# Top-32 attention with a PReLU layer on one core: four of nine selection masks on the scalar engine, output normalisation on GpSimd

## The chip, the core and the metric

The kernel runs on one core of one Trainium2 chip. A core has a matrix engine (PE, with PEld for its weight loads), a vector engine (DVE), a scalar engine (ACT), GpSimd (POOL) and a sync engine (SP) whose queue starts most transfers. Each engine works through its own list of instructions in order and waits on semaphores for the others. The metric is device time in microseconds (us): of several runs the median, and of one profiled run the trace.

## The reference, cut to what matters

```python
# q, k, v: (8, 8, 576, 64); tokens 4608, model width 512, hidden width 2048
scores = scale * q @ k^T                      # per batch and head, 576 x 576
kth    = 32nd largest score of each row
attn   = softmax(where(scores >= kth, scores, -1e9))
x      = (attn @ v) gathered to (4608, 512)
h      = x @ w_in
out    = (max(h, 0) + alpha * min(h, 0)) @ w_out
```

So each row of scores keeps its 32 largest entries; the rest get weight zero. The sum in the softmax is the sum of the kept exponentials, and a common factor on a row's kept weights falls out of the division.

## The kernel before, in words

Two heads make a **pair**: 32 pairs, four to a batch. A pair has nine score tiles of 128 rows by 576 columns (eight full ones, `j` 0 to 7, and `j` 8 that holds the last 64 rows of both heads). The 288 tiles are run by a loop written out by hand over **ticks**; tick `n` starts tile `n`, and in the same tick older tiles get their later steps. All five engines are ordered by this loop, with no scheduler behind it (`tc.manual_schedule`).

A tile's way through the engines:

- PE computes the scores into PSUM (L320). ACT copies them to SBUF with a per-row guess of the threshold subtracted (`b`, L329), then takes their sign with a running sum (`h`, L335; the sum `S_all` counts how many scores lie above the guess), and the exponential (`e`, L340), for two tiles at once where they come in twos.
- GpSimd turns the count into a sign word (`SG`, L345), one tick later. DVE flips the tile by it (`y`, L351), so that the wanted border lies among the small values, finds the eight largest of each of six segments (`C`, L361, two ticks after the tile's start), merges these to the 24 largest (`L`, L376 and L378, a tick later), and once for three tiles picks one of the 24 by rank (`sel_eq`, `sel_pr`, `sel_sum`; the rank comes from `sel_a`, L384, a square on ACT). `limit` (L405) turns it into the row's limit `KP`.
- Seven ticks after its start (`LAG_W`), a tile gets its mask on DVE (`mk = b >= KP`, L425). GpSimd multiplies mask and exponential to the weights (`w`, L435). SP transposes two tiles of weights at once by DMA (`wT`, L448).
- PE multiplies the transposed weights with v (`pu`, L486; `v` has a column of ones, so one column is the softmax sum): rows of `j` 0 to 3 as group 0, the rest as group 1. DVE takes the reciprocal of the sum (`rz`), and ACT writes the normalised outputs (`av_out`, L515): four activations of 64 columns for group 0, six for group 1. SP transposes those into `xT` (`x_turn`), and the hidden layer (L689 to L712) takes them from there, one step per tick.

Within a tick, DVE's order is: the masks, the held sum of a selection, the segments of one tile interleaved with the merge of another, small steps of the preparation of a later pair, `limit` every third tick, and last the flip of the tile before. GpSimd's order is: weights, then `SG`, then what the tick has at its end, among which are four DMA issues for `v` per pair (`load_v`, L149). A flip therefore needs the `SG` that GpSimd issues behind the weights of the same tick.

The masks use one buffer, the two-tile `b` five, the two-tile `e` four, `w2` three, `wT` six. The last four pairs run in another order of tiles with rules of their own.

## Time and profile before

| | |
|---|---|
| runs, us | 884.71, 878.32, 884.51 (median 884.51) |
| profiled run | 879.81 us, span of its instructions 878.0 us |
| DVE busy | 842.0 us, 5184 instructions |
| ACT busy | 771.2 us, 1841 instructions |
| PE busy | 738.2 us, 5771 matmuls; mean granted clock 0.896 |
| GpSimd busy | 526.6 us, 758 instructions |
| masks, L425 | 282 |
| weight products, L435 | 282 |
| output activations, L515 | 280 |

Busy time is the union of an engine's instructions. DVE and ACT begin an instruction before the one in front has quite ended, so the time from start to start is shorter than the duration in a row; for costs the starts count. Groups name an instruction by line, engine, operation and tiles, with how often it comes, its busy time and mean duration, then the idle time in front of it and what ended that. In a timeline the first column is the start in us, the second the time taken.

### The profile page before, as it was taken

How to read it: one execution, taken by the hardware profiler on the slowest of the kernel's cores; microseconds unless marked ns; L12 is line 12 of the kernel's file. 1: busy time of each engine (PE TensorE's matmuls, PEld its weight loads, DVE VectorE, ACT ScalarE, POOL GpSimd, SP SyncE). 2: the span in 40 equal slices, each digit the busy share in tenths (PEclk: the TensorE clock that was granted, in tenths of full speed). 3: DMA queues.
4: the chain of work that ended last, by engine and by line, in shares of the span. 5: the costliest groups of instructions: out<-in, count | busy, mean ns of one | idle time of the engine just before them, and what ended most of it. 6: DMA issues, size and time to landing. Idle time of an engine off the chain costs nothing.

```text
span 878.0 us, 20651 instructions
## 1 busy us (share of the span) xinstructions
PE 738.2 (84%) x5771; PEld 433.4 (49%) x5771; DVE 842.0 (96%) x5184; ACT 771.2 (88%) x1841; POOL 526.6 (60%) x758
## 2 busy tenths in 40 slices
PE   6776798778977889887987799988897888899996
PEld 4434444334554345544454445643455554566574
DVE  4999999999999999999999999999999999999992
ACT  6999989889997898999997988989988889889871
POOL 2676566666667656666567666666666665654530
PEclk8557679899978899899996989989999989999999
DMA  6999656655877556766566557575576663545442
GB/s 131 159 175 190 114 92 89 116 79 90 140 119 104 95 88 110 107 113 101 112 136 101 93 87 122 107 128 80 89 113 127 109 104 72 95 83 99 87 99 55
DMA packets 342619, 94.65 MB, mean 108 GB/s; under 512 B 334672, under 2 KB 334944, under 8 KB 342496
## 3 DMA queue, kind: packets, MB, share of 16 engines
q1 hardware_dynamic: 301232, 86.14, 52.8%
q0 software_dynamic: 40064, 6.82, 10.3%
q8 instruction: 47, 0.77, 0.4%
q14 instruction: 76, 0.62, 0.2%
q10 hardware_dynamic: 1200, 0.30, 0.2%
HBM read 36.71 MB, written 9.44 MB: 53 GB/s over the span
## 4 chain that ended last, share of the span: by engine, by line
DVE 67%; ACT 15%; PE 13%; DMA 2%; POOL 1%; issue 1%; SPq 0%; DVEq 0%
DVE C L361 22%; DVE y L351 10%; DVE mk L425 10%; DVE C L378 8%; DVE L L376 8%; PE ps L320 4%; ACT b L329 4%; PE pz L707 3%; ACT h L335 3%; ACT e L340 3%; DVE P L238 2%; PE ph L689 2%; ACT gT L695 2%; ACT xb L515 1%; DVE L L395 1%; DVE KK L399 1%
## 5 line engine op out<-in xcount | busy, mean ns | idle before, releaser
L435 POOL TENSOR_TENSOR w<-mk,e 128x576 bf16<-128x576 bf16 x250 | 318.8, 1275 | 253.8 <-DVE mk L425 146.8
L361 DVE MAX8 C<-y 128x8 f32<-128x96 f32 x1728 | 418.8, 243 | 0.1
L320 PE MATMUL ps<-qkT 64*128 64x288 f32 (+1 forms) x1280 | 262.8, 485 | 32.4 <-ACT b L329 32.1
L329 ACT ACTIVATE b<-ps,NT 128x576 f32<-128x576 f32 x288 | 202.2, 760 | 6.2 <-PE ps L320 6.0
L335 ACT ACTIVATE h<-b 128x576 bf16<-128x576 f32 x288 | 202.7, 704 | 1.6
L689 PE MATMUL ph<-xT,w_in_b 128*128 128x128 bf16 (+2 forms) x1024 | 156.3, 299 | 40.1 <-ACT gT L695 27.0
L320 PEld LDWEIGHTS ps<-qkT 64*128 64x128 f32 (+1 forms) x1280 | 138.8, 200 | 94.9 <-ACT b L329 57.1
L340 ACT ACTIVATE e<-b 128x1152 bf16<-128x1152 f32 (+1 forms) x158 | 173.8, 1100 | 0.0
L376 DVE MAX8 L<-C 128x8 f32<-128x48 f32 x864 | 162.5, 188 | 0.1
L351 DVE TENSOR_SCALAR y<-b,SG 128x576 int32<-128x576 int32 x288 | 149.4, 519 | 8.6 <-POOL SG L345 8.3
L425 DVE TENSOR_SCALAR mk<-b,KP 128x576 bf16<-128x576 f32 x282 | 148.0, 525 | 0.0
L707 PE MATMUL pz<-w_out_b,gT 128*128 128x512 bf16 x560 | 135.1, 380 | 0.0
L689 PEld LDWEIGHTS <-w_in_b 128*128 128x128 bf16 x1024 | 80.8, 100 | 108.8 <-issue 80.9
L695 ACT ACTIVATE gT<-ph 128x512 bf16<-128x512 f32 x140 | 85.7, 620 | 41.0 <-PE ph L689 40.8
L378 DVE MATCH_REPLACE8 C<-L,C 128x48 f32<-128x48 f32 x576 | 108.3, 188 | 0.0
L149 POOL DMA_DIRECT2D v_bf<-in_v_dram x128 | 101.8, 795 | 0.6 <-issue 0.3
L707 PEld LDWEIGHTS <-gT 128*128 128x128 bf16 x560 | 51.6, 98 | 68.5 <-issue 14.0
L486 PE MATMUL pu<-v_bf,wT 128*128 128x65 bf16 (+1 forms) x1600 | 69.6, 199 | 12.5 <-DMA wT<-w 8.2
L486 PEld LDWEIGHTS <-wT 128*128 128x128 bf16 (+1 forms) x1600 | 65.7, 104 | 22.9 <-issue 7.8
L345 POOL TENSOR_SCALAR SG<-S_all 128x1 int32<-128x1 f32 x288 | 64.5, 224 | 16.2 <-ACT h L335 16.0
L435 POOL TENSOR_TENSOR wm<-mk,e 128x576 bf16<-128x576 bf16 x32 | 40.8, 1275 | 47.5 <-DVE mk L425 44.7
L335 ACT ACTIVATION_READ_ACCUMULATOR h<-b 128x1 f32 x288 | 62.5, 217 | 0.0
(111 smaller groups left out, 762.8 us busy)
## 6 DMA issues: line engine op xcount, KB each, us to landing
out_dram<-o_sb SPq DMA_DIRECT2D x34, 256.0 KB, 2.4
st_q<-in_q_dram SPq DMA_DIRECT2D x64, 128.0 KB, 3.0
kst<-in_k_dram SPq DMA_DIRECT2D x62, 128.0 KB, 3.5
w_stage<-in_moe_w_out_dram SPq DMA_DIRECT2D x16, 256.0 KB, 3.5
v_bf<-in_v_dram POOLq DMA_DIRECT2D x64, 64.0 KB, 4.0
w_in_b<-in_moe_w_in_dram POOLq DMA_DIRECT2D x8, 256.0 KB, 6.5
wT<-w SPq DMA_TRANSPOSE x128, 3.6
st_q<-in_q_dram SPq DMA_DIRECT2D x32, 32.0 KB, 3.0
```

The lines of the kernel that those rows point to most:

```text
L320: nc.tensor.matmul(o_, l_, r_, start=True, stop=True)
L329: nc.scalar.activation(t["b"].rearrange("p (a c) -> p a c", a=2), t["ps"], AF.Identity, bias=NT0[:, p * TPP + j:p * TPP + j + 1], scale=ON ...
L335: nc.scalar.activation(h, tiles[n]["b"], AF.Sign, accum_out=S_all[:, n:n + 1])
L340: nc.scalar.activation(e, tiles[n0]["bu"], AF.Exp, scale=scl)
L351: nc.vector.tensor_scalar(t["y"].bitcast(I32), t["b"].bitcast(I32), FLIP, SG[:, n:n + 1], ALU.bitwise_xor, ALU.bitwise_xor)
L361: return [lambda g=g: nc.vector.max(out=C[:, n % TPP, g, :], in_=t["y"][:, g * SEG:(g + 1) * SEG]) for g in range(NSEG)]
L376: ops.append(lambda r=r, src=src: nc.vector.max(out=L[:, 8 * r:8 * r + 8], in_=src))
L378: ops.append(lambda r=r, src=src: nc.vector.match_replace(out=C2, in_to_replace=L[:, 8 * r:8 * r + 8], in_values=src, imm_value=NEG))
L425: nc.vector.tensor_scalar(t["mk"], t["b"], row_limit(n), None, ALU.is_ge)
L435: nc.gpsimd.tensor_tensor(dst, t["mk"], t["e"], ALU.mult)
L689: nc.tensor.matmul(hold[f][:, i, :], w_in_b[:, kk, (f + i) * 128:(f + i + 1) * 128], xT[:, kk, c0:c0 + tb], start=(kk == 0), stop=(kk == N ...
L707: nc.tensor.matmul(pz[0:m], hold["gT"][:, f, r0:r0 + m], w_out_b[:, f, :], start=False, stop=(f == NFT - 1))
```

## The change

Four tiles of a pair, `j` 0, 1, 4 and 5, are called late (all of them in pairs 0 to 26, two in pair 27, none in the last four: 110 tiles).

- A late tile's mask is no longer taken on DVE. ACT takes the sign of `b` plus the limit ten ticks after the tiles' start, and writes it as an unsigned byte into the upper half of each bf16 of one of three zeroed buffers. A kept entry is then the number 2^-125, any other zero. The exponential of these tiles is taken then too, with a bias that lifts it by 2^40.
- A late tile's weights come 11 (`j` 0, 1) or 12 ticks (`j` 4, 5) after its start, so each tick still has one weight product. In front of it DVE sets one element of the destination to zero (`mark`).
- The limits of the groups of three that hold late tiles change sign and are moved by a fraction of a last bit (`ulps`, `limit_2`: two more DVE instructions for 55 groups), so that a strict comparison keeps what "not smaller" kept.
- The rank's square moves from ACT to DVE as one instruction (96 times), a tick later.
- In pairs 0 to 26, ACT copies the unnormalised outputs from PSUM to SBUF (one instruction for group 0, two for group 1), and GpSimd multiplies them with the reciprocals, two heads at once: two products of 128 columns for group 0, three for group 1. They are issued at the end of a tick, behind `SG`: those of group 0 eight ticks, those of group 1 eight (five for the last pair of a batch) after the weights that complete the group.
- PE takes up a group two ticks after its last weights (before: three for group 0, four for group 1), and the transposes of a batch's outputs and the hidden layer's start move accordingly.

```diff
+    def late(n):
+        p, j = ORDER[n]
+        return p < P0 and (j in (0, 1) or j in (4, 5) and p < P0 - 1)
+
+    def act_w(n0):
+        for i in range(2):
+            t = tiles[n0 + i]
+            t["mk"] = mk8s[late_at[n0 + i] % NM8]
+            nc.scalar.activation(
+                t["mk"].bitcast(U8).rearrange("p (s two) -> p s two", two=2)[:, :, 1], t["b"],
+                AF.Sign, bias=row_limit(n0 + i), scale=1.0)
+        e = attn.tile([128, 2, S], BF16, name="e2", bufs=4)
+        nc.scalar.activation(e, tiles[n0]["bu"], AF.Exp, bias=lift, scale=scl)
...
     def sel_a(m):
         a = attn.tile([128, 3], FP32, name="ra", bufs=2)
-        nc.scalar.activation(a, S_all[:, 3 * m:3 * m + 3], AF.Square, bias=c513)
+        sm = S_all[:, 3 * m:3 * m + 3]
+        nc.vector.scalar_tensor_tensor(out=a, in0=sm, scalar=1026.0, in1=sm, op0=ALU.add,
+                                       op1=ALU.mult)
...
     def limit(m):
         ms = slice(3 * m, 3 * m + 3)
         KPs[m] = attn.tile([128, 3], FP32, name="KP", bufs=4)
+        if nudged(m):
+            ulps[m] = attn.tile([128, 3], FP32, name="ulp", bufs=2)
+            nc.vector.tensor_scalar(ulps[m].bitcast(I32), KK[:, ms].bitcast(I32), -1, EXPO,
+                                    ALU.bitwise_xor, ALU.bitwise_and)
...
+    def limit_2(m):
+        nc.vector.scalar_tensor_tensor(out=KPs[m], in0=ulps.pop(m), scalar=ULP, in1=KPs[m],
+                                       op0=ALU.mult, op1=ALU.add)
...
     def mask(n):
         t = tiles[n]
         t["mk"] = attn.tile([128, S], BF16, name="mk", bufs=1)
-        nc.vector.tensor_scalar(t["mk"], t["b"], row_limit(n), None, ALU.is_ge)
+        if nudged(n // 3):
+            nc.vector.tensor_scalar(t["mk"], t["b"], row_limit(n), 0.0, ALU.add, ALU.is_gt)
+        else:
+            nc.vector.tensor_scalar(t["mk"], t["b"], row_limit(n), None, ALU.is_ge)
+
+    def mark(n):
+        d, j = w_dst(n), ORDER[n][1]
+        nc.vector.memset(d[:, 0:1], 0.0)
+        tiles[n]["dst"] = d
...
+    def av_copy(p, g):
+        d = pairs[p]
+        pu = d["pu", g]
+        d["cp", g] = cp = attn.tile([128, 6, D], FP32, name="cp", bufs=1)
+        nc.scalar.copy(cp[:, 0:4, :], pu[:, 0:4, 0:D])
+        if g == 1:
+            nc.scalar.copy(cp[0:64, 4:6, :], pu[0:64, 4:6, 0:D])
+
+    def gp_out(p, g):
+        b, kt = p // KPB, p % KPB
+        cp, rz = pairs[p]["cp", g], pairs[p]["rz", g]
+        for i in range(2 + g):
+            m = 128 if i < 2 else 64
+            dst = xb[b][2 * g + i] if i < 2 else xm[b]
+            nc.gpsimd.tensor_tensor(
+                dst[:, 128 * kt:128 * kt + 128].rearrange("p (s d) -> p s d", s=2),
+                cp[0:m, 2 * i:2 * i + 2, :],
+                rz[0:m, 2 * i:2 * i + 2].unsqueeze(2).to_broadcast([m, 2, D]), ALU.mult)
...
-                if wj == 3:
-                    put(n + 3, "pe", lambda: av(wp, 0))
-                    put(n + 4, "dve", lambda: av_rz(wp, 0))
-                    put(n + 6, "act", lambda: av_out(wp, 0))
+                new = wp < P0 - 1
+                if wj == 1:
+                    put(n + 2, "pe", lambda: av(wp, 0))
+                    put(n + 3, "dve", lambda: av_rz(wp, 0))
+                    if new:
+                        put(n + 4, "act", lambda: av_copy(wp, 0))
+                        put(n + 8, "end", lambda: gp_out(wp, 0))
...
-                if wj == 8:
-                    put(n + 4, "pe", lambda: av(wp, 1))
-                    put(n + 5, "dve", lambda: av_rz(wp, 1))
-                    put(n + 7, "act", lambda: av_out(wp, 1))
+                if wj == (5 if new else 8):
+                    put(n + 2, "pe", lambda: av(wp, 1))
+                    put(n + 3, "dve", lambda: av_rz(wp, 1))
+                    if new:
+                        dx = 5 if wp % KPB == KPB - 1 else 8
+                        put(n + 5, "act", lambda: av_copy(wp, 1))
+                        put(n + dx, "end", lambda: gp_out(wp, 1))
...
+            lag = LAG_W if not late(wn) else 11 if ORDER[wn][1] < 2 else 12
+            wdue.setdefault(wn + lag if wn < NW else 3 * (wn // 3) + 7, []).append(wn)
...
+                    if not late(n0):
+                        act_e(n0)
+            if n - 10 in unit_of and unit_of[n - 10][2] == 0 and late(n - 10):
+                act_w(n - 10)
...
             for wn in due:
-                if wn < NW:
+                if late(wn):
+                    mark(wn)
+                elif wn < NW and len(due) == 1:
                     mask(wn)
...
             for wn in due:
-                weights(wn, wn >= NW)
+                weights(wn, wn >= NW or len(due) > 1 and not late(wn))
```

More of the change, by code (lines that the diff above doesn't have):

```diff
@@ L78 @@
     iota = const.tile([128, KW], FP32, name="iota")
-    c513 = const.tile([128, 1], FP32, name="c513")
-    nc.gpsimd.memset(c513, 513.0)
+    lift = const.tile([128, 1], FP32, name="lift")
+    nc.gpsimd.memset(lift, LIFT)
     w_in_b = const.tile([128, NKT, DFF], BF16, name="w_in_b")
@@ L112 @@
     v_bfs = [prep.tile([128, 10, V1], BF16, name=f"v_bf{i}", bufs=1) for i in range(NV)]
+    mk8s = [prep.tile([128, S], BF16, name=f"mk8_{i}", bufs=1) for i in range(NM8)]
     NQ = 5
@@ L120, in early_sets @@
             nc.gpsimd.memset(ksts[i][64:128, 4, :], 0.0)
+        for t_ in mk8s:
+            nc.gpsimd.memset(t_, 0.0)
         for t_ in v_bfs:
@@ L125, in early_sets @@
         for i in range(KW):
-            nc.vector.memset(iota[:, i:i + 1], (1.0 + 2 * i) ** 2)
+            nc.vector.memset(iota[:, i:i + 1], (1.0 + 2 * i) ** 2 - 513.0 ** 2)
     pairs = {}
@@ L342, in act_e @@
             tiles[n0 + i]["e"] = e[:, i, :]
+    def late(n):
[10 more added lines that the diff above has]
+        nc.scalar.activation(e, tiles[n0]["bu"], AF.Exp, bias=lift, scale=scl)
+        for i in range(2):
+            tiles[n0 + i]["e"] = e[:, i, :]
     def side_of(n):
@@ L400, in sel_sum, with nudged @@
                                 axis=mybir.AxisListType.X)
+    ulps = {}
+    def nudged(m):
+        return any(late(n) for n in range(3 * m, 3 * m + 3))
     def limit(m):
@@ L429, in weights @@
         d, t = pairs[p], tiles.pop(n)
-        dst = w_dst(n)
+        dst = t["dst"] if "dst" in t else w_dst(n)
         if fused:
@@ L743 @@
         cal = {}
+        late_at = {x: i for i, x in enumerate(x for x in range(NT) if late(x))}
         def put(tick, eng, f):
@@ L886 @@
                 side_of(n - 1)
+            if n >= 4 and n % 3 == 1 and n - 4 < NT:
+                sel_a((n - 4) // 3)
             segs = seg_ops(n - LAG_S) if 0 <= n - LAG_S < NT else []
@@ L906 @@
             run(n, "dvx")
+            if lm // 3 in ulps:
+                limit_2(lm // 3)
             if pick:
```

32 lines of the change are left out of this document (19 added, 13 removed).

## The prediction

> **What bounds the kernel now.** I read the page first: the busy time of each engine, the slices, the chain that ended last, the costly groups.
>
> ```profile
> span 878.0 us, 20651 instructions
> PE 738.2 (84%) x5771; PEld 433.4 (49%) x5771; DVE 842.0 (96%) x5184; ACT 771.2 (88%) x1841; POOL 526.6 (60%) x758
> ...
> DVE  4999999999999999999999999999999999999992
> ...
> DVE 67%; ACT 15%; PE 13%; DMA 2%; POOL 1%; issue 1%; SPq 0%; DVEq 0%
> DVE C L361 22%; DVE y L351 10%; DVE mk L425 10%; DVE C L378 8%; DVE L L376 8%; PE ps L320 4%; ACT b L329 4%; PE pz L707 3%; ACT h L335 3%; ACT e L340 3%; DVE P L238 2%; PE ph L689 2%; ACT gT L695 2%; ACT xb L515 1%; DVE L L395 1%; DVE KK L399 1%
> ...
> L435 POOL TENSOR_TENSOR w<-mk,e 128x576 bf16<-128x576 bf16 x250 | 318.8, 1275 | 253.8 <-DVE mk L425 146.8
> ```
>
> DVE is the bound: nine tenths or more in every slice but the first and the last, and two thirds of the chain that ended last. GpSimd is idle for much of the time, but half of its 253.8 us in front of the products ended when a mask did. Next I cut the span into stretches of nine tiles (one pair each, from flip to flip over eight pairs) and asked for busy times.
>
> ```profile
> core 0: us, PE busy (x) PEld busy (x) DVE busy (x) ACT busy (x) POOL busy (x), PEclk, DMA share, GB/s
> ...
> 331.00:356.90 25.90, 25.08 (x264) 16.40 (x261) 25.90 (x162) 24.98 (x61) 16.51 (x24) 1.00 0.64 117
> ...
> 382.80:408.60 25.80, 20.07 (x158) 11.09 (x158) 25.80 (x161) 25.02 (x62) 16.43 (x24) 1.00 0.55 86
> ...
> 460.40:487.50 27.10, 21.78 (x151) 13.31 (x151) 27.10 (x167) 21.88 (x57) 19.68 (x28) 0.74 0.73 113
> ...
> sum 208.50, PE 178.09 PEld 101.00 DVE 208.46 ACT 190.24 POOL 134.87; mean PE 22.26 PEld 12.63 DVE 26.06 ACT 23.78 POOL 16.86
> ```
>
> DVE has no gap at all; a pair takes 25.9 us but for the one of 27.1. ACT is not far behind: 25.02 us of a pair's 25.80 where the hidden layer feeds it, 21.88 in the lightest, 190.24 of 208.50 over the eight. So what DVE saves counts in full only down to about 25 us per pair.
>
> Last, one tick in the timeline, which shows what hangs on what.
>
> ```profile
> 406.10 0.51 DVE L351 TENSOR_SCALAR y<-b,SG 128x576 int32<-128x576 int32 x1
> ...
> 406.53 0.51 DVE L425 TENSOR_SCALAR mk<-b,KP 128x576 bf16<-128x576 f32 x1
> ...
> 406.96 0.25 DVE L361 MAX8 C<-y 128x8 f32<-128x96 f32 x1
> ...
> 407.13 1.27 POOL L435 TENSOR_TENSOR w<-mk,e 128x576 bf16<-128x576 bf16 x1 [1.23 <-DVE mk L425]
> ...
> 408.38 0.23 POOL L345 TENSOR_SCALAR SG<-S_all 128x1 int32<-128x1 f32 x1
> ...
> 408.43 2.18 SPq L448 DMA_TRANSPOSE wT<-w  x1
> ...
> 408.56 0.92 POOL L149 DMA_DIRECT2D v_bf<-in_v_dram  x1
> 408.65 0.52 DVE L351 TENSOR_SCALAR y<-b,SG 128x576 int32<-128x576 int32 x1
> 409.08 0.66 DVE L425 TENSOR_SCALAR mk<-b,KP 128x576 bf16<-128x576 f32 x1
> ...
> 411.31 0.60 POOL L149 DMA_DIRECT2D v_bf<-in_v_dram  x1
> ```
>
> From start to start a flip takes 0.43 us (406.10 to 406.53) and a mask 0.43. The product starts 0.60 after the mask's start (407.13), `SG` 1.25 later (408.38), and the flip 0.27 behind that (408.65). So from mask to flip GpSimd's chain takes 2.12 us, DVE's own work also 2.12 (0.43, then 1.69 of scanning and merging from 406.96 to 408.65). **The two are even**: whatever delays GpSimd's product by more than a few hundredths of a us delays the flip, and so the bound.
>
> **The change part by part: DVE.** The masks that go: 110 x 0.43 = 47.3 us. What comes:
>
> ```profile
> 14.30 0.52 DVE L351 TENSOR_SCALAR y<-b,SG 128x576 int32<-128x576 int32 x1 [3.34 <-POOL SG L345]
> 14.86 1.06 DVE L361 MAX8 C<-y 128x8 f32<-128x96 f32 x6
> ...
> 28.19 0.14 DVE L405 SCALAR_TENSOR_TENSOR KP<-KK,SG 128x3 int32<-128x3 int32 x1
> 28.25 0.51 DVE L351 TENSOR_SCALAR y<-b,SG 128x576 int32<-128x576 int32 x1
> ```
>
> A small instruction is followed by the next after 0.06 us (28.19 to 28.25). At that price: 110 `mark`s 6.6 us, 96 `sel_a` 5.8, 55 `ulp`s and 55 `limit_2` 6.6. Without a mask behind it, a flip is followed by the scan of its own result, and that starts 0.56 after the flip (14.30 to 14.86), not 0.43 + 0.06; for `j` 0 and `j` 5 nothing else lies between: 55 x 0.07 = 3.9. A mask right behind `limit_2` must wait for it to end (0.14 in the row of 28.19, less the 0.06): `j` 3, 27 x 0.1 = 2.7. Two products of mask and exponential that fall into one tick at the change to the last four pairs are negligible. Sum: 47.3 - 25.6 = **21.7 us saved**, 0.8 per pair: 25.1 instead of 25.9. The mark is bounded by zero and 0.06.
>
> ```profile
> L441 POOL TENSOR_TENSOR wm<-mk,e 128x64 bf16<-128x64 bf16 x32 | 9.8, 306 | 0.0
> ...
> L126 DVE MEMSET iota<- 128x1 f32 x24 | 0.4, 59 | 0.0
> ```
>
> The 24 memsets to one element took 59 ns each and 0.4 us in all, so back to back far less; the low end would save 6 us more.
>
> **GpSimd.** It gains 27 x 5 = 135 products of 128 columns, of fp32 against a column spread over 64. The trace has none like it. From 576 columns in 1275 ns and 64 in 306: 1.89 ns per column, so 427 ns, back to back some 0.4; if twice the bytes cost twice, 0.85; not below the 0.31 of half the columns. I take 0.42, since the rows differ in width alone. That is 57 us of an engine with 351 idle. But **place** counts. A late tile's product can start 0.15 after its tiny `mark` instead of 0.60 after a mask, so GpSimd has its `SG` ready some 0.2 us before DVE needs it, and then has only the flip's 0.43 and 0.15 until the next product wants to start. Two ticks per pair put products there:
>
> - Behind the tick of `j` 0: two products and a short `v` issue (0.60, 411.31), then the weights of `j` 1. `SG` comes -0.2 + 0.84 + 0.60 + 1.25 + 0.27 = 2.76 us after the flip; DVE needs it after 0.43 + 0.14 (`sel_pr`) + 0.06 + 0.14 (`sel_sum`) + 1.69 + 0.06 = 2.52. Late by 0.24.
> - Behind the tick of `j` 4: three products, then the weights of `j` 5: -0.2 + 1.26 + 1.25 + 0.27 = 2.58 against 0.56 + 1.69 + 0.13 (`sel_eq`) = 2.38. Late by 0.20, in three pairs of four; the last of a batch has them before a masked tick, where a product starts at 1.03 or later and they fit.
>
> That is 0.24 + 0.15 = 0.39 per pair if the products run undisturbed. They won't quite: they start with the flip, while before only `v` issues ran there. In the tick above, an issue of 0.92 us (408.56) lies across a mask that takes 0.66 instead of 0.51. And a rare overlap of a two-input DVE instruction with a GpSimd product:
>
> ```profile
> 44.14 1.38 POOL L435 TENSOR_TENSOR w<-mk,e 128x576 bf16<-128x576 bf16 x1
> 44.17 0.22 DVE L389 TENSOR_TENSOR EQ<-ra,iota 128x72 f32<-128x72 f32 x1
> ```
>
> The product took 1.38 instead of 1.28, the DVE instruction its usual 0.2. So the two engines do slow each other, by about the DVE instruction's time. If the flip (0.43) and `sel_pr` (0.14) are paid by the products: 0.57 + 0.75 x 0.43 = 0.89 more per pair. Bounds 0.39 and 1.28; I take the middle, 0.84, since the one overlap seen paid 0.10 of 0.13. Times 27: **22.7 us lost** (10.5 to 34.6). The Trainium skill, "SBUF — State Buffer", section "Who interferes with whom", says the pair of ports that VectorE and GpSimd share is locked for a whole instruction and the loser fully blocks, for fp32 `tensor_scalar` among others. The overlap above is no full block; by the Trainium skill's rule the sum would take the upper bound.
>
> **ACT.**
>
> ```profile
> 303.46 0.30 ACT L384 ACTIVATE ra<-S_all,c 128x3 f32<-128x3 f32 x1
> 303.65 0.60 ACT L695 ACTIVATE gT<-ph 128x512 bf16<-128x512 f32 x1
> 304.13 0.69 ACT L335 ACTIVATE h<-b 128x576 bf16<-128x576 f32 x1
> 304.70 0.21 ACT L335 ACTIVATION_READ_ACCUMULATOR h<-b 128x1 f32 x1
> ...
> 320.32 0.29 ACT L212 COPY qkT<-pt 128x128 f32<-128x128 f32 x1
> 320.47 0.95 ACT L515 ACTIVATE xb<-pu,rz 128x64 bf16<-128x64 f32 x4
> 321.27 1.21 ACT L340 ACTIVATE e<-b 128x1152 bf16<-128x1152 f32 x1
> ```
>
> Starts again: a sign 0.57 (304.13 to 304.70), a square 0.19, a copy of 128 columns out of PSUM 0.15, an output activation 0.20 (four in 0.80). Added: 110 signs with a per-row bias, 0.57 to 0.63, 63 to 69 us; 27 copies of 256 columns twice (some 0.25 each between 0.15 and the 0.47 of 512) and 128: 17.6. Gone: 270 outputs, 54; 96 squares, 18. Net +9 to +15 us, 0.3 to 0.5 per pair. The full pairs go from 25.0 to 25.4 busy, below the 25.9 - 0.8 + 0.84 that DVE and GpSimd would allow. No price, but the idle left is its cover.
>
> **PE and the transposes.** Fewer ticks lie between weights and PE:
>
> ```profile
> 414.83 0.81 PE L486 MATMUL pu<-v_bf,wT 128*128 128x65 bf16 x20
> ```
>
> ```profile
> wT<-w SPq DMA_TRANSPOSE x128, 3.6
> ```
>
> In the tick above the product that completes `j` 2, 3 starts at 407.13, its transpose is issued at 408.43, and PE takes the group up at 414.83, in the third tick. The median from issue to landing is 3.6 us, so 412.0: 2.8 us of room; one tick less is 2.9, with 0.45 given back by the earlier product. That room is used up. I price it at nothing, since a PE wait costs only when ACT then runs dry, and list it below.
>
> **The sum.** 879.8 - 21.7 + 22.7 = 880.8 against the profiled run. The median of the runs is 4.7 higher (two of three near 884.6, one at 878.3), so 881 to 885.5; I say **884 us**. No change can be told from one within 1%.
>
> **The rivals.**
>
> *GpSimd's products fit* (faster). The flip may go through without cost to them, as the 0.52 of 408.65 did beside an issue. Then 879.8 - 21.7 + 10.5 = 868.6, on the median 873; with marks near zero and products at 0.31, 858. For it: GpSimd's idle share of 40%. Against: the even chains of the tick.
>
> *The flip and the products block each other* (slower). Place: ticks of `j` 0 and 4; price 34.6: 892.7, on the median 897. It decides once a product costs over 0.4 and pays for the flip. The Trainium skill's rule ("SBUF — State Buffer", "Who interferes with whom") leads here. For it speaks the 0.66 us mask, against it the 0.22 of `sel_eq` beside a product.
>
> *ACT and PE become the bound* (slower). A late tile's product needs two signs and an exponential made in the same tick of ACT, 0.57 x 2 + 1.2 after the sign sum that the flip at that tick's end wants as well.
>
> ```profile
> 406.15 0.70 ACT L335 ACTIVATE h<-b 128x576 bf16<-128x576 f32 x1
> ...
> 411.57 0.59 DVE L351 TENSOR_SCALAR y<-b,SG 128x576 int32<-128x576 int32 x1
> ```
>
> Here ACT ended its sum (406.85) 4.7 us before the flip that uses it; needed will be 2.4 + 1.25 + 0.3 = 4.0. And PE's lost room pulls the other way: an ACT too far ahead waits for transposes. If ACT keeps its idle of 18.3 us in eight pairs and adds 0.5 per pair, these take 212.5 instead of 208.5: +16 us, 896 to 901. It decides if less than a quarter of that idle can be used.
>
> *The byte signs cost more* (the change doesn't do what it says). A byte at every second place is not in the trace; at twice 0.57, +63 us on ACT, some 930.
>
> **How the numbers follow.** Forecast 0.33, fit 0.32, block 0.18, ACT and PE 0.13, byte signs 0.04. Range: the fit's lower half is reached at 862, block and ACT at 904; 2 in 10 stay out. The forecast's own range is 876 to 893. Faster by over 1%: the fit and a little, 0.33; within: 0.31; slower: the three others and part of the forecast, 0.36.
>
> **What would show it.** About 170 masks; DVE's instructions per pair worth 25.1 us. Right: idle before flips released by `SG`, in the ticks behind products, 0.5 to 1.2 us per pair. Products near 0.42 us. Signs near 0.7 us of duration. Wrong: flips without such waits and a span near 860 (fit); long waits of products on ACT, or of PE on `wT`, and ACT over 95% busy (ACT and PE); signs of a us or more.

## The result and the profile after

The changed kernel took **939.4 us** (median of 4 runs, 933.05 to 947.77) against 882.43 (878.32 to 884.71) for the kernel before: a ratio of **1.063, 95% interval 1.055 to 1.071**, some 57 us slower. The forecast of 884 us and its range of 862 to 904 were wrong; slower had been given a chance of 0.36. The profiled run (947.77 us) is the longest of the four and counts as a slow one (its granted clock was 0.873, in the others 0.888 to 0.904), so waits read from its trace are rather too long, and what a cause is worth is taken from timed runs.

The head of the page of the changed kernel (busy time of each engine, its share of the span, instructions):

```profile
span 946.0 us, 20915 instructions
...
PE 767.5 (81%) x5771; PEld 434.8 (46%) x5771; DVE 853.1 (90%) x5390; ACT 801.1 (85%) x1666; POOL 581.0 (61%) x894
```

Before, DVE was busy for 842.0 us of 878.0 and so idle for 36.0. Now it is busy for 853.1 and idle for 92.9. Both numbers speak against the forecast: 110 masks have left DVE, yet its sum rose by 11 us, and 57 us of waiting came on top.

What DVE and ACT waited for (view of waits; microseconds in all, times, longest):

```profile
engine line waited for: us in total, times, longest us
DVE P L246 <- PE pr L238: 41.8, 22, 4.2
DVE y L375 <- POOL SG L369: 9.9, 8, 3.2
DVE rz L550 <- PE pu L533: 9.1, 3, 8.2
```

```profile
ACT cp L558 <- POOL xm L568: 34.5, 20, 2.9
```

Of DVE's idle time 41.8 us lie ahead of one instruction: `P`, which needs PE's `pr` of the next pair's preparation (2.6 before). And ACT, in whose waits GpSimd did not appear before, now stands 20 times in 27 pairs, 34.5 us in all, ahead of its copy into `cp`, behind the product of `xm`. How the one makes the other, in order of time (start, duration, engine, line, operands, in brackets the wait ahead of it):

```profile
487.73 0.98 POOL L568 TENSOR_TENSOR xb<-cp,rz 128x128 bf16<-128x128 f32 x2
...
488.67 0.39 POOL L568 TENSOR_TENSOR xm<-cp,rz 64x128 bf16<-64x128 f32 x1
...
489.10 0.37 ACT L558 COPY cp<-pu 128x256 f32<-128x256 f32 x1 [2.63 <-POOL xm L568]
489.36 1.17 ACT L348 ACTIVATE e<-b 128x1152 bf16<-128x1152 f32 x1
...
491.21 2.29 PE L328 MATMUL ps<-qkT 64*128 64x288 f32 x6 [2.28 <-ACT b L337]
...
496.10 0.69 PE L238 MATMUL pr<-qkT,GK 64*64 64x512 bf16 x4
...
496.78 0.82 DVE L246 TENSOR_TENSOR P<-pr,qkT 128x512 bf16<-128x512 f32 x2 [3.33 <-PE pr L238]
...
498.89 1.27 POOL L482 TENSOR_TENSOR w<-mk,e 128x576 bf16<-128x576 bf16 x1 [4.91 <-DVE mk L465]
```

The three products of a pair's second group end at 489.06. Only then can ACT copy the next pair's first group, since `cp` has **one buffer** and the products still read it: ACT has stood for 2.63 us with its exponential (489.36) and the whole tick's work behind that copy. Its copy of the scores (`b`) is late by as much, so PE stands for 2.28 us ahead of the next scores (491.21); PE's `pr`, behind those and other work in PE's list, follows at 496.10, and DVE stands 3.33 us ahead of `P`. GpSimd in turn waits 4.91 us for a mask.

The groups that the forecast had priced (busy, mean of one in ns, idle time ahead), after:

```profile
L360 ACT ACTIVATE mk<-b,KP 128x576 uint8<-128x576 f32 x110 | 79.9, 785 | 0.0
...
L364 ACT ACTIVATE e<-b,lift 128x1152 bf16<-128x1152 f32 x55 | 69.2, 1258 | 0.0
L467 DVE TENSOR_SCALAR mk<-b,KP 128x576 bf16<-128x576 f32 x115 | 58.7, 510 | 0.0
L568 POOL TENSOR_TENSOR xb<-cp,rz 128x128 bf16<-128x128 f32 x108 | 49.9, 482 | 0.0
...
L415 DVE TENSOR_TENSOR EQ<-ra,iota 128x72 f32<-128x72 f32 x96 | 36.2, 377 | 0.0
...
L465 DVE TENSOR_SCALAR mk<-b,KP 128x576 bf16<-128x576 f32 x55 | 28.4, 517 | 1.0
```

and three of DVE's as they were before:

```profile
L425 DVE TENSOR_SCALAR mk<-b,KP 128x576 bf16<-128x576 f32 x282 | 148.0, 525 | 0.0
...
L389 DVE TENSOR_TENSOR EQ<-ra,iota 128x72 f32<-128x72 f32 x96 | 19.7, 205 | 0.0
...
L266 DVE TENSOR_SCALAR t<-sq 128x9 int32<-128x9 int32 x32 | 5.2, 162 | 0.1
```

The masks have gone from 282 to 55 + 115 (two more fell to fused instructions). A product took 0.48 us, a byte sign 0.79, the exponential made with the signs 1.26 (before, at the same width: 1.19). `EQ`, the selection's comparison on DVE, which the change touches only in its constants, went from 205 ns to 377: 16.5 us more.

### The profile page after: what moved, and what is told of

It is laid out like the page before. It is cut to its first block, busy times and chain, and to the rows that moved or that the text cites. A ratio compares the mean times of both kernels' runs of the same rounds, so it can differ in the third digit from the quotient of the medians.

```text
span 946.0 us, 20915 instructions
## 1 busy us (share of the span) xinstructions
PE 767.5 (81%) x5771; PEld 434.8 (46%) x5771; DVE 853.1 (90%) x5390; ACT 801.1 (85%) x1666; POOL 581.0 (61%) x894
## 5 line engine op out<-in xcount | busy, mean ns | idle before, releaser
L385 DVE MAX8 C<-y 128x8 f32<-128x96 f32 x1728 | 423.4, 245 | 1.4
L328 PE MATMUL ps<-qkT 64*128 64x288 f32 (+1 forms) x1280 | 268.5, 491 | 49.6 <-ACT b L337 49.0
L375 DVE TENSOR_SCALAR y<-b,SG 128x576 int32<-128x576 int32 x288 | 153.8, 534 | 16.0 <-POOL SG L369 9.9
L400 DVE MAX8 L<-C 128x8 f32<-128x48 f32 x864 | 164.7, 191 | 0.1
L773 PE MATMUL pz<-w_out_b,gT 128*128 128x512 bf16 x560 | 144.7, 400 | 0.0
L348 ACT ACTIVATE e<-b 128x1152 bf16<-128x1152 f32 (+1 forms) x103 | 107.4, 1043 | 2.9 <-POOL w L482 2.9
L157 POOL DMA_DIRECT2D v_bf<-in_v_dram x128 | 98.4, 769 | 1.3 <-issue 0.8
L533 PE MATMUL pu<-v_bf,wT 128*128 128x65 bf16 (+1 forms) x1600 | 69.5, 199 | 18.3 <-DMA wT<-w 17.2
L360 ACT ACTIVATE mk<-b,KP 128x576 uint8<-128x576 f32 x110 | 79.9, 785 | 0.0
L364 ACT ACTIVATE e<-b,lift 128x1152 bf16<-128x1152 f32 x55 | 69.2, 1258 | 0.0
```

Source lines behind the costliest of these rows:

```text
L328: nc.tensor.matmul(o_, l_, r_, start=True, stop=True)
L348: nc.scalar.activation(e, tiles[n0]["bu"], AF.Exp, scale=scl)
L375: nc.vector.tensor_scalar(t["y"].bitcast(I32), t["b"].bitcast(I32), FLIP, SG[:, n:n + 1], ALU.bitwise_xor, ALU.bitwise_xor)
L385: return [lambda g=g: nc.vector.max(out=C[:, n % TPP, g, :], in_=t["y"][:, g * SEG:(g + 1) * SEG]) for g in range(NSEG)]
L400: ops.append(lambda r=r, src=src: nc.vector.max(out=L[:, 8 * r:8 * r + 8], in_=src))
L533: nc.tensor.matmul(o_, wT[:, 4 * side + c, cs], d["v"][:, 5 * side + c, :], start=(c == 0), stop=(c == 4))
```

## The experiments

Each run was timed beside the kernel before on the same chip, which took 879 to 881 us there. In the short diffs "-" is the kernel named as the base.

### The one copy buffer

**e1_early5**, on the changed kernel: the second group's products come five ticks after its last weights in every pair, as they did in the last pair of a batch, so they end well ahead of the next copy.

```
-                        dx = 5 if wp % KPB == KPB - 1 else 8
+                        dx = 5
```

> The products of group 1 come five ticks after the weights in all pairs, not eight, so that the single buffer cp is free three ticks before ACT wants it again. Theory (the one buffer makes ACT wait for GpSimd): the 34.5 us that ACT's copies waited for GpSimd go, and with them most of the 41.8 us in which DVE waited for PE's pr; 885 to 900 us. Rival (DVE's two-input instructions are held up by GpSimd's products): only a third of the products move to a better place, 925 to 935 us. Rival (the late masks themselves cost it): 930 to 940 us.

**e2_bf16x2**, on the changed kernel: two buffers, in bf16 so that they take the room of one.

```
-        d["cp", g] = cp = attn.tile([128, 6, D], FP32, name="cp", bufs=1)
+        d["cp", g] = cp = attn.tile([128, 6, D], BF16, name="cp", bufs=2)
```

> cp in bf16 and two buffers of it in the same space, all places as in the changed kernel; the unnormalised outputs are rounded once more. Theory (one buffer): ACT's waits at the copies go, 885 to 900 us. Rivals (held-up DVE instructions, or the late masks): 930 to 940 us, as the products stay where they are.

Measured: 895.7 us (ratio 1.018, 1.014 to 1.023) and 896.05 (1.019, 1.017 to 1.020). Two different ways of taking the buffer out of the way give the same back. The waits of ACT ahead of `cp` and of DVE ahead of `P` in e1_early5:

```profile
ACT cp L558 <- DVE rz L550: 4.9, 4, 1.4
```

```profile
DVE P L246 <- PE pr L238: 2.4, 5, 1.1
```

The wait for `xm` is gone (in e2_bf16x2 too, where 4.6 us of waiting for `rz` stand in the same place), and DVE waits 2.4 us for `pr`, as before the change. So **about 40 of the 57 us are the single buffer**: 39 by the ratios (1.063 less 1.018, of 880), 43.7 by the medians. Left are 16, though four of nine masks have gone from DVE.

### The two halves of the change apart

**e3_masks**, on the changed kernel: late masks as there, but the outputs are scaled on ACT as before; no copy, no product.

```
-                    if new:
-                        put(n + 4, "act", lambda: av_copy(wp, 0))
-                        put(n + 8, "end", lambda: gp_out(wp, 0))
+                    put(n + 4, "act", lambda: av_out(wp, 0))
...
-                        put(n + dx, "end", lambda: gp_out(wp, 1))
+                    put(n + 5, "act", lambda: av_out(wp, 1))
```

> Late masks, limits and the square as in the changed kernel, but the outputs stay on ACT as scaled activations, two ticks after PE; no copy, no GpSimd product. Theory (one buffer): no wait for GpSimd; DVE saves its 21 us, but ACT has 0.20 x 270 less 17.6, that is 36 us, more than in the changed kernel, 805 + 36 = 837 busy, so ACT bounds it: 885 to 905 us. Rival (held-up DVE instructions): the products are gone, below 880 us. Rival (late masks): 930 us or more.

**e4_outs**, on the kernel before: only the outputs change hands, copied by ACT and multiplied by GpSimd. The turn of the first rows of the late batches, and the feeding behind it, come three ticks later (not shown).

```
-                    put(n + 6, "act", lambda: av_out(wp, 0))
+                    put(n + 6, "act", lambda: av_copy(wp, 0))
+                    put(n + 8, "end", lambda: gp_out(wp, 0))
...
-                    put(n + 7, "act", lambda: av_out(wp, 1))
+                    put(n + 7, "act", lambda: av_copy(wp, 1))
+                    put(n + 7, "end", lambda: gp_out(wp, 1))
```

> The kernel before with its masks, and only the outputs through a copy on ACT and products on GpSimd, the products of group 0 eight and of group 1 seven ticks after the weights that complete them, so that cp is free in time. Theory (one buffer): same as before within 1%, 875 to 890 us. Rival (held-up DVE instructions): 900 us or more. Rival (late masks): 875 to 890 us.

**e8_copy**, on the kernel before: ACT's copies alone, straight into the output tile, in the places of e4_outs and without products. The division by the softmax sum is left out.

```
-                    put(n + 6, "act", lambda: av_out(wp, 0))
+                    put(n + 6, "act", lambda: av_copy(wp, 0))
...
+            nc.scalar.copy(
+                dst[:, 128 * kt:128 * kt + 128].rearrange("p (s d) -> p s d", s=2),
+                pu[0:m, 2 * i:2 * i + 2, 0:D])
```

> The kernel before with the outputs only copied by ACT (the division left out), no products on GpSimd. Theory (products hold DVE up, 20 us): as before, 874 to 882 us, since DVE does the same work without being held up, though ACT has 30 us less to do. Rival (the changed places of the outputs cost the 20 us): 895 us or more.

Measured: 917.58 (1.046, 1.041 to 1.051), 898.76 (1.023, 1.021 to 1.025) and 881.66 (0.998, 0.995 to 1.000). Each half loses by itself. The masks alone lose more than I expected. The products alone cost some 20 us, which the theory of the buffer had not foreseen; the rival (DVE held up by the products) had. The heads of e3_masks and e4_outs, and two of DVE's groups in e4_outs, neither of which touches the outputs:

```profile
span 915.8 us, 20961 instructions
...
PE 741.8 (81%) x5771; PEld 429.8 (47%) x5771; DVE 826.8 (90%) x5390; ACT 834.8 (91%) x1855; POOL 526.3 (57%) x759
```

```profile
span 895.8 us, 20620 instructions
...
PE 732.0 (82%) x5771; PEld 434.2 (48%) x5771; DVE 861.0 (96%) x5184; ACT 741.7 (83%) x1652; POOL 581.5 (65%) x893
```

```profile
L425 DVE TENSOR_SCALAR mk<-b,KP 128x576 bf16<-128x576 f32 x282 | 153.9, 546 | 0.0
...
L266 DVE TENSOR_SCALAR t<-sq 128x9 int32<-128x9 int32 x32 | 10.7, 336 | 0.1
```

In e4_outs DVE has the same 5184 instructions as before and is busy for 861.0 us instead of 842.0. The masks take 546 ns instead of 525, and `t`, nine elements wide, 336 instead of 162. With the flips (532 instead of 519) and `km`, a product in the preparation of a pair (248 instead of 139), these groups make 18.8 of the 19.0 us. In e3_masks, without products, DVE is down to 826.8, but ACT is up to 834.8 of 915.8, and DVE waits. e8_copy, where ACT's work falls to 742.8 us, gains nothing: the kernel before was not bound by ACT. Nor is it the moved places of the outputs that cost e4_outs its 20 us, since e8_copy has the same places.

### Signs and products, on and off

Which of them holds the 16 us that are left? Four runs make a table with e1_early5.

**e5_noprod**, on the changed kernel: ACT copies into the output tile, no products (the edit of `av_copy` is that of e8_copy; the division is left out here too).

```
-            nc.gpsimd.tensor_tensor(
+            nc.scalar.copy(
                 dst[:, 128 * kt:128 * kt + 128].rearrange("p (s d) -> p s d", s=2),
-                cp[0:m, 2 * i:2 * i + 2, :],
-                rz[0:m, 2 * i:2 * i + 2].unsqueeze(2).to_broadcast([m, 2, D]), ALU.mult)
+                pu[0:m, 2 * i:2 * i + 2, 0:D])
```

> The changed kernel without GpSimd's products and without cp: ACT copies the outputs straight to their place, so the division by the softmax sum is left out. Theory now (one buffer for cp, and besides it GpSimd and DVE shutting each other out): both are gone, DVE keeps its 20 us, 860 to 872 us. Rival (the wait of GpSimd's late product for ACT's exponential, which is the last thing ACT makes in a tick): that wait stays, 875 to 890 us. Rival (products cost only through the buffer): about the 895 of the run with two buffers.

**e10_nosign** is e5_noprod, and **e13_nosign_prod** is e1_early5, with the signs taken out. The mask buffers then hold a constant 1, so the masks of the late tiles are not formed:

```
-            nc.gpsimd.memset(t_, 0.0)
+            nc.gpsimd.memset(t_, 1.0)
...
-            nc.scalar.activation(
-                t["mk"].bitcast(U8).rearrange("p (s two) -> p s two", two=2)[:, :, 1], t["b"],
-                AF.Sign, bias=row_limit(n0 + i), scale=1.0)
```

> As the run without products and without the fp32 copies (e5_noprod, 892.9; the division of the attention outputs is left out there), and the 110 byte signs of ACT are left out too: the mask buffers hold a constant 1, so four of nine masks of a pair are not formed at all. ACT loses 110 x 0.67 = 74 us of work. Theory 'ACT is now the bound of the late positions': the 12 us above the kernel before go and the 20 us of DVE's saving show, 858-872. Rival 'it is order and latency (the weights and PE two ticks behind), not ACT's sum': 883-893.

> As the run with the early products (e1_early5, 895.7), with the 110 byte signs of ACT left out (the mask buffers hold a constant 1, so four of nine masks of a pair are not formed); the products of GpSimd stay. Theory 'two losses that add: ACT's sum sets the pace, and products hold DVE up': the run without signs and without products took 854.7, plus some 15-20 for the products: 868-878. Rival 'the hold-up by the products mattered only because DVE had to wait for late data': 853-863. Rival 'ACT is not the bound while the products stay': 885-896.

**e15_sign45** and **e16_sign01**, on e1_early5: half of the signs, `(4, 5)` kept in the one (shown), `(0, 1)` in the other.

```
+            if ORDER[n0][1] in (4, 5):
                 nc.scalar.activation(
                     t["mk"].bitcast(U8).rearrange("p (s two) -> p s two", two=2)[:, :, 1], t["b"],
```

> As the run with the early products (e1_early5), with the byte signs of the first two tiles of a pair left out and those of the fifth and sixth kept (two of nine masks of a pair are not formed). If it is ACT's sum that costs, half of the signs gives half of what all give (that run, e13_nosign_prod, is in the same call): 880-888 where all give 870. If the place costs (the first two tiles' weights are due in the tick after their sign), nearly all of it: 868-878.

> The other half: the byte signs of the fifth and sixth tile of a pair left out, those of the first two kept. If ACT's sum costs: 880-888, as the run beside it. If the place costs: 888-896, hardly better than with all signs.

Measured, in us:

| | all signs | (4, 5) only | (0, 1) only | no signs |
|---|---|---|---|---|
| with products | 895.7 | 885.8 | 886.8 | 885.2 |
| without | 892.9 | | | 854.7 |

The ratios to the kernel before are 1.013 (1.009 to 1.017) for e5_noprod, 0.969 (0.964 to 0.973) for e10_nosign, 1.003 (1.000 to 1.005) for e13_nosign_prod, 1.005 (1.003 to 1.008) and 1.006 (1.003 to 1.008) for the two halves. **The losses don't add.** Taking out the products alone gives 3 us (no more than the intervals leave open), the signs alone 10, both 41 (4, 14 and 44 by the ratios). Each of the two holds the time at 885 to 893 by itself. My expectation for e5_noprod was wrong both ways, that for e13_nosign_prod fell to its third rival, and the halves gave neither half of the gain nor a difference of place: with products there, half of the signs is free wherever it stands. The profiled runs show why in part: in e1_early5 DVE is busy for 849.6 us and idle for 47.4, in e5_noprod for 826.7 and 61.2. With the signs in place the products add 22.9 us to DVE's work, but 13.8 of them take the place of waiting.

The heads of e5_noprod, e10_nosign and e13_nosign_prod show what each is bound by:

```profile
span 887.9 us, 20800 instructions
...
PE 726.1 (82%) x5771; PEld 425.4 (48%) x5771; DVE 826.7 (93%) x5390; ACT 801.4 (90%) x1720; POOL 525.2 (59%) x759
```

```profile
span 853.6 us, 20665 instructions
...
PE 727.9 (85%) x5771; PEld 422.9 (50%) x5771; DVE 813.9 (95%) x5390; ACT 731.9 (86%) x1610; POOL 525.4 (62%) x759
```

```profile
span 885.1 us, 20737 instructions
...
PE 721.2 (81%) x5695; PEld 418.9 (47%) x5771; DVE 842.5 (95%) x5390; ACT 732.1 (83%) x1556; POOL 576.8 (65%) x894
```

- e10_nosign: DVE is busy for 813.9 of 853.6 us. That is 28.1 less than before the change, the saving that the change was to bring, and here the span follows it (24.4 less).
- e13_nosign_prod has the same 5390 instructions on DVE, and ACT is busy for as long (732.1). DVE is busy for **28.6 us more**, and the span is 31.5 longer: the products cost time by making DVE's own instructions longer.
- e5_noprod: ACT is busy for 801.4 instead of 731.9. DVE's sum is 12.8 higher and its idle time 61.2 instead of 39.7: 34.3 in all, the difference of the spans.

Which instructions of DVE get longer, in e10_nosign and then in e13_nosign_prod:

```profile
L412 DVE TENSOR_TENSOR EQ<-ra,iota 128x72 f32<-128x72 f32 x96 | 19.9, 207 | 0.0
...
L274 DVE TENSOR_SCALAR t<-sq 128x9 int32<-128x9 int32 x32 | 5.4, 169 | 0.1
...
L271 DVE TENSOR_TENSOR sq<-M,sq 128x9 f32<-128x9 f32 x32 | 4.9, 152 | 1.2 <-ACT M L267 1.2
```

```profile
L412 DVE TENSOR_TENSOR EQ<-ra,iota 128x72 f32<-128x72 f32 x96 | 33.4, 348 | 0.0
...
L274 DVE TENSOR_SCALAR t<-sq 128x9 int32<-128x9 int32 x32 | 10.8, 336 | 0.1
L271 DVE TENSOR_TENSOR sq<-M,sq 128x9 f32<-128x9 f32 x32 | 10.6, 331 | 1.0 <-ACT M L267 1.0
```

`EQ`, `t` and `sq` make 13.5 + 5.4 + 5.7 = 24.6 of the 28.6 us. In e5_noprod `EQ` is long as well, beside the weight product that waits for a late exponential. The timelines of e13_nosign_prod, with each of the three, and of e1_early5:

```profile
207.70 0.74 POOL L565 TENSOR_TENSOR xb<-cp,rz 128x128 bf16<-128x128 f32 x2
207.75 0.80 DVE L412 TENSOR_TENSOR EQ<-ra,iota 128x72 f32<-128x72 f32 x1
```

```profile
161.51 0.74 POOL L565 TENSOR_TENSOR xb<-cp,rz 128x128 bf16<-128x128 f32 x2
...
161.56 0.37 DVE L271 TENSOR_TENSOR sq<-M,sq 128x9 f32<-128x9 f32 x1
...
162.01 0.57 DVE L372 TENSOR_SCALAR y<-b,SG 128x576 int32<-128x576 int32 x1
...
162.23 0.60 POOL L565 TENSOR_TENSOR xm<-cp,rz 64x128 bf16<-64x128 f32 x1
...
162.50 0.37 DVE L274 TENSOR_SCALAR t<-sq 128x9 int32<-128x9 int32 x1
```

```profile
420.43 1.45 ACT L360 ACTIVATE mk<-b,KP 128x576 uint8<-128x576 f32 x2
...
421.76 1.26 ACT L364 ACTIVATE e<-b,lift 128x1152 bf16<-128x1152 f32 x1
...
423.16 1.27 POOL L482 TENSOR_TENSOR w<-mk,e 128x576 bf16<-128x576 bf16 x1 [1.46 <-ACT e L364]
...
423.22 1.30 DVE L415 TENSOR_TENSOR EQ<-ra,iota 128x72 f32<-128x72 f32 x1
```

`EQ` starts 0.05 us after a pair of products, takes 0.80 instead of 0.21 and ends when the second one has ended (208.55 against 208.44). `sq` slips in between the two products of its pair, after 0.37 instead of 0.15. The `xm` product starts while the flip runs (162.01) and takes 0.60 instead of the 0.39 that it took at 488.67 above, so here GpSimd pays; `t`, the next on DVE, starts 0.27 us after that product and ends 0.04 after it. In e1_early5 the weight product waited 1.46 us for ACT's exponential and so came to lie on `EQ`, which took **1.30 us**, to 0.09 after the product's end. DVE's small instruction is shut out until GpSimd's instruction ends. The Trainium skill, "SBUF — State Buffer", section "Who interferes with whom", says just this: a DVE instruction with two inputs in SBUF contends with a GpSimd instruction that reads SBUF, and what they contend for is an exclusive lock. The traces agree, with 1.30 us.

### Moving the work out of each other's way

If it is a matter of which instructions meet, moving them should help. Eight runs moved signs, copies or products. None gained clear of the intervals.

**e9_order**, on e1_early5: the second sign behind the exponential (first diff). **e6_sign9**, on e1_early5: signs and exponential a tick earlier (second diff). **e7_noprod9**: e6_sign9 without products.

```
+            if i == 0:
+                nc.scalar.activation(e, tiles[n0]["bu"], AF.Exp, bias=lift, scale=scl)
-        nc.scalar.activation(e, tiles[n0]["bu"], AF.Exp, bias=lift, scale=scl)
```

> As the run with the early products (e1_early5), with one swap: of the two late tiles of a pair of tiles, the second one's byte sign is issued after the exponential instead of before it. The exponential that the first weight product waits for then starts one sign (0.67 us from start to start) earlier. Theory 'late exponentials set the pace' (GpSimd w waits for ACT's exponential and the selection's comparison on DVE then lies beside the product and is shut out, 1.30 us once): 55 times up to 0.3-0.67 us at position 0 of nine, so 16-37 us of waiting, of which about a third on the path: 883-892. Rival 'only the products hold DVE up': the exponential's place is free, 893-899.

```
-            if n - 10 in unit_of and unit_of[n - 10][2] == 0 and late(n - 10):
-                act_w(n - 10)
+            if n - 9 in unit_of and unit_of[n - 9][2] == 0 and late(n - 9):
+                act_w(n - 9)
```

> Group 1's products five ticks after the weights, and ACT takes the late signs and exponentials nine ticks after the tiles' start, not ten. Theory (GpSimd's weights of j 0 wait for ACT's exponential, and a selection step on DVE is shut out for the rest of that product): the step in that tick falls from some 590 ns to its 130 to 220, the tick from 3.1 to 2.6 us, 27 x 0.5 = 13 us less than without: 880 to 886 us. Rival (only GpSimd's products hold DVE up): no change, 893 to 898 us.

> Both: no products (the division left out) and the signs nine ticks after the start. Theory: what masks alone are worth when nothing is in their way, 25.1 us per pair on DVE: 855 to 865 us. Rival (ACT bounds it): ACT is busy some 800 us and must wait for PE besides, 870 us or more.

**e12_pe3**, on e1_early5, and **e11_sign9_pe3**, on e6_sign9: PE's product, the reciprocal and the copies a tick later, and with them the second group's products. **e14_copy_late**: of these only the copies and the products (the first two lines stay as they were).

```
-                    put(n + 2, "pe", lambda: av(wp, 0))
-                    put(n + 3, "dve", lambda: av_rz(wp, 0))
-                        put(n + 4, "act", lambda: av_copy(wp, 0))
+                    put(n + 2 + new, "pe", lambda: av(wp, 0))
+                    put(n + 3 + new, "dve", lambda: av_rz(wp, 0))
+                        put(n + 5, "act", lambda: av_copy(wp, 0))
...
-                        dx = 5
-                        put(n + 5, "act", lambda: av_copy(wp, 1))
+                        dx = 6
+                        put(n + 6, "act", lambda: av_copy(wp, 1))
```

> As the run with the early products (e1_early5, 895.7), and PE's second attention product, the reciprocal and the copy of the output one tick later, nothing else. If PE's distance of two ticks behind the late weights costs time there, 885-892; if not, 893-899. The products of a group then come right behind their copy, so up to 5 us more if GpSimd's list is what is late.

> As the run with ACT's signs and exponential one tick earlier (e6_sign9, 920.1), and PE's second attention product, the reciprocal and the copy of the output one tick later. Theory 'that run lost its gain to DVE's reciprocal, which waited 44.6 us for PE's product': with a tick more that wait goes, 875-890. Rival 'the earlier signs delay ACT's gT and qkT copies and so PE (70.9 and 33.2 us there)': 905-920, the waits of PE stay.

> As the run with the early products (e1_early5, 895.7), with only ACT's copies of the attention outputs (and the second group's products) one tick later; PE's product and the reciprocal stay where they were. The run that moved all three took 942.6. If the copies' place in ACT's list was it: 930-945. If it was the place of PE's product: 893-900.

**e17_prod_place**, on e13_nosign_prod: the first group's products a tick earlier. **e18_best**, on e9_order: that, and the second group's a tick later (the line of `dx`).

```
-                        put(n + 8, "end", lambda: gp_out(wp, 0))
+                        put(n + 7, "end", lambda: gp_out(wp, 0))
...
-                        dx = 5
+                        dx = 6
```

> As the run without byte signs and with products (e13_nosign_prod, 885.2; four of nine masks of a pair are not formed), with one edit: GpSimd's products of the first group are issued one tick earlier, so that they no longer lie beside the selection's comparison on DVE, which took 0.80 us in 25 of its 96 runs there against 0.21 otherwise (348 ns in the mean). Theory 'GpSimd's products shut DVE's two-input instructions out until they end': the comparison falls to about 205 ns in the mean (13.5 us less), and up to 5 us come back at the flip of the tick before: 871-880. Rival 'GpSimd's longer list makes something else late': no change, 883-887.

> As the run with the swapped sign and exponential (e9_order, 894.2; nothing left out), with the products of both groups moved: the first group's one tick earlier, the second's one tick later, so that neither lies beside the comparison nor beside the two instructions of the next pair's preparation (L271, L274: 331 and 337 ns against 147 and 162 before). Theory 'shut out by the products': up to 13 + 9 us of DVE's time, of which some is put back elsewhere since ACT bounds the ticks of the late signs: 880-890. Rival 'with the signs kept ACT alone sets the pace': 892-897.

Measured:

| run | us | ratio (95%) | the base |
|---|---|---|---|
| e9_order | 894.2 | 1.014 (1.008 to 1.020) | 895.7 |
| e6_sign9 | 920.13 | 1.042 (1.037 to 1.046) | 895.7 |
| e7_noprod9 | 915.74 | 1.037 (1.033 to 1.041) | 920.13 |
| e12_pe3 | 942.58 | 1.073 (1.065 to 1.080) | 895.7 |
| e11_sign9_pe3 | 934.4 | 1.059 (1.055 to 1.064) | 920.13 |
| e14_copy_late | 908.46 | 1.030 (1.024 to 1.036) | 895.7 |
| e17_prod_place | 887.73 | 1.008 (1.006 to 1.011) | 885.2 |
| e18_best | 912.2 | 1.036 (1.032 to 1.041) | 894.2 |

In e9_order the time stayed, as its rival said. e6_sign9 lost 24 us where I had expected a gain, and e7_noprod9, without products, hardly less: DVE's reciprocal `rz` now waits for PE, as the view of waits of e6_sign9 shows (57.9 us in e7_noprod9), and giving PE a tick more (e11_sign9_pe3) cuts that wait and brings another, of the flip `y` for `SG`:

```profile
DVE rz L550 <- PE pu L533: 44.6, 27, 9.1
```

```profile
DVE y L375 <- POOL SG L369: 40.8, 27, 3.3
DVE rz L550 <- PE pu L533: 18.5, 10, 5.1
```

The clearest is e17_prod_place, where only the products moved. `EQ` fell from 348 ns to 298 and the flip rose from 518 to 527:

```profile
L372 DVE TENSOR_SCALAR y<-b,SG 128x576 int32<-128x576 int32 x288 | 151.7, 527 | 9.7 <-POOL SG L366 6.3
...
L412 DVE TENSOR_TENSOR EQ<-ra,iota 128x72 f32<-128x72 f32 x96 | 28.6, 298 | 0.0
```

DVE is busy for 842.9 us, 842.5 in its base. `EQ` no longer meets products; in 24 of its 96 runs it now waits for the next weight product, mostly for 0.62 us in all. With products in its list GpSimd is busy for 581 of 883 us instead of 525 of 854, and what leaves one of DVE's instructions falls on another. I had expected the time to fall; it didn't, and **moving one product only moved the hold-up**.

e14_copy_late and e18_best lost 13 and 18 us, e12_pe3 47. In all three the turn of a finished batch and the feeding of its dense layer also come a tick later (they hang on `dx`), and PE's loads for `ph` stand for longer without a wait that the profile shows (115 to 126 us in all, 90.6 in e1_early5). But e6_sign9, where the turn stays in its place, has 119.0 of these too. Whether that, ACT's order or DVE's waits for `rz` weighs most was not separated; why a single tick costs so much there stays **open**.

## Why the prediction was wrong, point by point

- **DVE's saving (21.7 us forecast): right in kind, and too small.** e10_nosign, where little disturbs DVE, has 28.1 us less on DVE than before.
- **Products on GpSimd (22.7 us lost, bounds 10.5 to 34.6): the size was near, by luck, and the mechanism wrong.** DVE's sum grows by 19.0 us (e4_outs) and by 28.6 (e13_nosign_prod). The price was worked out as lateness of `SG` and as DVE's flip paid by GpSimd. In fact `SG` is hardly late (9.9 us of waits for it, 8.3 before), and it is DVE that pays: `EQ`, `sq`, `t`, in e4_outs masks and flips too, shut out by a product or stretched beside it. The forecast took its one overlap (0.22 us beside a product) as evidence that there is no full block. It was a block the other way round: `EQ` began 0.03 us after the product's start and went first, and the product waited. In the traces of all runs, `EQ` went first in all 17 cases in which it began up to 0.054 us after a weight product, which then lasted 1.35 to 1.40 us instead of 1.27, and ended behind the product in every case in which it began later.
- **ACT (+9 to +15 us, "No price, but the idle left is its cover"): this is the step that failed,** in three ways. Its size: ACT's busy time rose by 29.9 us (771.2 to 801.1); a sign took 0.79 us, and in the timeline of e1_early5 the starts of two signs and of the exponential behind them lie 1.33 apart (420.43 to 421.76), 0.67 each instead of 0.57 to 0.63. Its cover: without products, the signs add 69.5 us to ACT's work (801.4 against 731.9) and cost 38 us (892.9 against 854.7), so the idle time covered only about half; the wait of a weight product for ACT's exponential (1.46 us at 423.16) is one place where it did not. And above all a wait that I did not list: the copy that I counted among ACT's additions writes a tile with **one buffer**, which GpSimd's products, that my own working had placed behind the tick of `j` 4, hold. The forecast followed these products into GpSimd's list and not back to ACT. That one argument, `bufs=1`, is about 40 of the 57 us.
- **PE and the transposes (no price):** the room was used up as said; DVE's waits for `rz` on PE are small in the changed kernel (9.1 us) but were what the moved runs fell over (44.6 in e6_sign9).
- **The rivals.** "Block each other" (897, chance 0.18) has the mechanism. Its time fits once the buffer is out of the way (895.7), but that is luck: with the products and without the signs it is 885.2. "ACT and PE become the bound" (896 to 901, 0.13) is there as well: the signs without the products give 892.9. Either alone uses up DVE's saving, and the two together give 895.7. "Products fit" (0.32) is refuted by e4_outs, "byte signs cost more" by 0.79 us. None of the rivals had the buffer, which took the time out of the range.
- **What would show it.** "Idle before flips released by `SG`" was to be the sign of the forecast; there is next to none. "Long waits of products on ACT, or of PE on `wT`" was to show the ACT rival; the wait that came is the reverse, of ACT on products.

## What to carry to other kernels

Where a step is handed to another engine through a new tile, look up that tile's buffers, and follow its reader back to its next writer: the price is not the reader's work but what stands behind the writer in its queue. Two costs that each fill the same slack don't add: undo them one at a time and both together (here 3, 10 and 41 us), or each looks harmless. And a saving on DVE that puts elementwise work on GpSimd has to be weighed with DVE's small two-input instructions beside it; moving the products by a tick here moved the hold-up and removed none of it.

## What the runs showed of the hardware

- A GpSimd product of two tensors in SBUF shuts out a DVE instruction with two tensor inputs until it ends: a comparison of 72 columns took 1.30 us instead of 0.2, a subtraction of 9 elements 0.37 instead of 0.15. A `tensor_scalar` on 9 int32 elements (`t`, 336 against 169 ns), which has one tensor input, is hit too. Two products in a row keep DVE out for both in the case of the comparison (0.80).
- Who comes first decides, but the starts in the trace tell it only to some hundredths of a us: 0.03 us after the start of a weight product the comparison took 0.22 and the product paid 0.10 (kernel before, 44.14 and 44.17), up to 0.054 it still went first, and from 0.055 on it waited. Beside the output products of the runs the order could go either way from 0.03 us before the product's start to 0.04 after it (once 0.11).
- A sign written to every second byte, with a bias per row, costs ACT 0.67 us from start to start for 576 columns; a square of three columns that was taken from it had cost 0.19.
- A product of 128 fp32 columns with a column spread over 64 took 0.74 us for two in a row (207.70), so about 0.37 each, below the 0.42 of the forecast.
